# A second set of cell tiles, a planner fed with measured lengths, moved x tiles and paired output pieces in a fused retention and two-MLP kernel

## The chip, the cores and the metric

The kernel runs on one core of a Trainium2 chip. The metric is device time in microseconds (us), the median of several executions; lower is better. Durations inside the kernel come from one profiled execution.

## The reference, cut to what matters

Retention (linear attention with a decay per head) over 4 x 8 heads of 576 tokens, then two MLPs on the 2304 tokens that result, all in float32:

```python
ret = scores * Dmat            # scores = q k^T / 8, Dmat = gamma ** (i - j), lower triangle
x = (ret @ v)                  # 2304 tokens x 512
h = np.maximum(x @ w_in, 0.0)  # first MLP, 512 -> 2048 -> 512
x = h * h @ w_out
g = x @ w_gate                 # second MLP, 512 -> 1536 -> 512
out = g / (1 + exp(-g)) * (x @ w_val) @ w_out2
```

The weights arrive as float64 (the host only views them as 64-bit integers) and are rounded to float32 on the chip.

## The kernel before

Every float32 product is three TensorE matmuls: both operands are split into a high part, which is exact in the matmul's rounded format, and a low rest, and `three` (lines 188 to 190) adds high x high, high x low and low x high in PSUM.

**Tiles and stages.** The 2304 tokens are 18 cells of 128. Five token blocks (`BLOCKS`) of 4, 2, 4, 4 and 4 cells go through the first MLP.

- Start: the first four cells go through retention; PE fills planned idle time with matmuls on zeros (`fill`, line 1150).
- Stage 1: the plain blocks 0 (512 tokens) and 1 (256 tokens). For each of the 16 steps f of a block PE does 12 matmuls `h` (`mlp1_h`, into `hps`) and, one step later, 12 matmuls `y` (`mlp1_y`, into `acc`). After some of these steps one retention cell is inserted (`INSERTS`): `att_out` does I (previous state times q), K (sums k^T v, into `hps`) and O (decayed scores times v), and `att_scores` then does S, the scores of the next cell. Before, ten cells (4 to 13) stand in block 0, after f = 1, 3, 5, 7, 9, 11, 12, 13, 14, 15, and four in block 1. The scores of cell 4 stand directly ahead of its own I, K, O.
- Stage 2: blocks 2 to 4 by seven block products in place of eight (`mlp1_s`, `PRODUCTS`), eight double steps p a block. The moving operands are the `xb` tiles (256 columns); the seven products of a double step are followed in pairs by 512-column pieces of `y`.
- Stage 3: the second MLP in two-level form, 36 steps (`mlp2_gv`): seven products of six 384-column matmuls (`xc` tiles) a step, and six output pieces (`mlp2_o`, lines 1076 to 1078, 512 columns) of earlier steps, placed by `other(i)`: one piece before product 0, one after each of products 1 to 4, one after product 6, so that a lone piece stands on both sides of products 2 to 5, and two pieces stand together where one step meets the next.

**Cells and their tiles.** A cell needs three loads: `qk` (A, 512 KB), `kv` (V, 512 KB) and `qt` (Q, 256 KB), into one set of tiles in the pool `up`. The load of A for cell c waits for S and the q scaling (POOL, line 465) of cell c-1, Q for I of c-1, V for O and K of c-1. A cell's output is saved to DRAM (`xd`) from cell 6 on; all these saves stand ahead of the point `open`, from which stage 2's tiles take the room of the cells' tiles. `fetch_x1(2)` loads the first such block into `xs` and splits it into the seven `xb` tiles on ACT and DVE.

**Weights.** `round32` and `convert1` turn a raw 1 MB load into a split weight tile `w` (ACT lines 229, 234, 267; DVE lines 237, 240, 246, 249, 271); even ones are also stored to `wf` and later come back to `convert_s`, which forms the sums of the block products on POOL (line 337) and stores them in `ws`. Stage 2 converts the second MLP's weights (`convert_gv`, `convert_out`) to DRAM (`wdP`, `wdS`, `wdO`), from which stage 3 loads them through a ring of seven tiles.

**Order.** PE's order is written out by hand (`pe` chains each group to the one before). All other engines, SP (which issues the DMAs) included, get their order from `Plan`: a list scheduler that runs through the program with a length for each operation, takes for each engine the operation that is ready first, by rank, and emits it. The chip then runs each engine's queue in that order: an instruction, or a DMA issue, that has to wait holds up everything behind it on its engine. A DMA's planned landing is

```python
lanes = max(lanes, t + o.us + 1.3) + o.kb / 400.0
o.end = lanes + 0.5
```

**Addresses.** `pad` tiles shift what follows them. `x` of block 1 and the 256-column `h` tiles begin 192 bytes (`shift`, 48 floats) past a multiple of 1,024. The `xb` tiles follow the pools `pad2` to `tl` and `pad3`, which together put all their 1,024-byte parts at a multiple of 1,024.

In stage 3, product 6 writes the bank `MA` again and so waits for `c22` (DVE, line 1001), which reads product 4 from it.

Of the kernel before, what the change touches and what calls it, by code (L numbers as in the profile page):

```python
# [51 lines left out]
INSERTS = {0: (1, 3, 5, 7, 9, 11, 12, 13, 14, 15), 1: (1, 3, 5, 7)}  # L52
# [13 lines left out]
class Plan:  # L66
# [20 lines left out]
    def emit(self):  # L87
# [11 lines left out]
        while left:  # L99
# [45 lines left out]
def kernel(ctx: ExitStack, tc: tile.TileContext, units, qtab, tab, w1, w2, out):  # L145
# [24 lines left out]
    tl = ctx.enter_context(tc.tile_pool(name="tl", bufs=1))  # L170
    ctx.enter_context(tc.tile_pool(name="pad3", bufs=1)).tile([128, 80], F32, name="pad3")
# [50 lines left out]
    def round32(box, rank):  # L222
# [30 lines left out]
        p1 = do("DVE", 0.69, d1, [o1], rank)  # L253
        p2 = do("DVE", 0.69, d2, [p1], rank)
        p3 = do("DVE", 0.69, d3, [p2, o2], rank)
# [3 lines left out]
        p4 = do("DVE", 1.22, d4, [p3, o2], rank)  # L259
# [64 lines left out]
    def convert_s(p, rank):  # L324
# [16 lines left out]
        x = do("POOL", 0.67, add(2, 3, 2, ALU.add), [ld], rank)  # L341
        x = do("POOL", 0.67, add(3, 0, 3, ALU.subtract), [x], rank)
        x = do("POOL", 0.67, add(0, 2, 0, ALU.subtract), [x], rank)
        x = do("POOL", 0.67, add(1, 1, 0, ALU.subtract), [x], rank)
# [11 lines left out]
    def sums(st, deps, rank):  # L356
# [10 lines left out]
        s = do("POOL", 0.67, add(0, a21, a22, ALU.add, True), [*deps, *r_users[-1:]], rank)  # L367
        s = do("POOL", 0.67, add(1, 0, a11, ALU.subtract), [s], rank)
        s = do("POOL", 0.67, add(2, a11, a21, ALU.subtract), [s], rank)
        return do("POOL", 0.67, add(3, a12, 1, ALU.subtract), [s], rank)  # L370
# [23 lines left out]
    astack = ExitStack()  # L394
    xp = astack.enter_context(tc.tile_pool(name="xp", bufs=1))
# [29 lines left out]

    def att_load(c, rank):

        def go_a():
            A[c] = up.tile([128, NP, 2, C], F32, tag="qk", name="qk")
            nc.sync.dma_start(out=A[c], in_=units[c, 0])  # L430

        def go_b():
            V[c] = up.tile([128, NP, 2, C], F32, tag="kv", name="kv")
            nc.sync.dma_start(out=V[c], in_=units[c, 1])

        def go_q():
            Q[c] = up.tile([128, NP, C], F32, tag="qt", name="qt")
# [3 lines left out]
        A_op[c] = do("SP", 0.45, go_a, [S_op[c - 1], qs_op[c - 1]] if late_cell else (), rank, kb=512, after=[A_op[c - 1]])  # L441
        if c not in FIRST:
            Q_op[c] = do("SP", 0.45, go_q, [I_op[c - 1 - (c - 1 in FIRST)]] if late_cell else (), rank, kb=256, after=[Q_op[c - 1]])
        V_op[c] = do("SP", 0.45, go_b, [O_op[c - 1], K_op[c - 1]] if late_cell else (), rank, kb=512, after=[V_op[c - 1]])
# [11 lines left out]
    def att_prep(c, rank):  # L456
# [10 lines left out]
        if c not in FIRST:  # L467
            qs_op[c] = do("POOL", 1.3, qs, [A_op[c], Q_op[c]], rank, after=[ks_op[c - 1]])
        if c not in LAST:
            ks_op[c] = do("POOL", 1.15, ks, [V_op[c], tab_op], rank, after=[qs_op[c]])  # L470
# [23 lines left out]
    def att_out(c, rank, steps, fill=None, deps=()):  # L494
# [220 lines left out]
    def sum_loads():  # L715
# [5 lines left out]
        for n, (j, p, name, i) in enumerate(order):  # L721
# [4 lines left out]
            def go(j=j, p=p, name=name, k=k):  # L726
                if k == NF1P and "sx" not in late:
                    late["sx"] = late["xs"].tile([128, 2, HALF1], F32R, tag="sx", name="sx")
                SB[j, p, name] = t = Wt[2 * k][:, :, 3 * HALF1:] if k < NF1P else late["sx"]
# [13 lines left out]
    def mlp1_s(j, p, pieces):  # L743
# [58 lines left out]
        def finish(key, f, half, deps):  # L802
# [556 lines left out]
```

## Time and profile before

| | us |
|---|---|
| median of 3 runs (lowest, highest) | 932.97 (932.87, 933.08) |
| profiled execution, its own time | 934.24 |
| its span, first to last instruction | 932.5 |
| TensorE matmul (PE) busy | 895.4 |
| VectorE (DVE) busy | 561.7 |
| ScalarE (ACT) busy | 429.7 |
| GpSimd (POOL) busy | 193.0 |
| DMA, mean over the span | 253 GB/s |
| mean granted TensorE clock | 0.989 of full |

A share of busy time is a mean over the whole span; the stages have different limits. The start of a matmul to the start of the next is its price, since matmuls are pipelined and a row's duration overlaps the next one's. PE = TensorE matmul, SPq = the queue that issues DMAs.

### The profile page before, as it was taken

Reading aid. Unit: us, or ns where it says so; the run is one execution under the profiler, and the core shown is the slowest. Engines: PE = TensorE matmul, PEld = TensorE weight load, DVE = VectorE, ACT = ScalarE, POOL = GpSimd, SP = SyncE. Lnnn points to the kernel's source line nnn. Section 1 sums busy time; section 2 is a strip of 40 time slices with the busy share of each in tenths; the row PEclk is TensorE's granted clock in tenths of the full one; section 3 lists DMA queues with packets and bytes.
Section 4 is the critical chain, followed back from the end, with each engine's and each line's share of the span. In section 5 each row is a group of like instructions: output and inputs, shape, how many; then the busy total and the mean of one; then the engine's idle time right before and its main releaser. Section 6 shows DMA issues by size and latency. Waiting matters only on the chain.

```text
span 932.5 us, 14460 instructions
## 1 busy us (share of the span) xinstructions
PE 895.4 (96%) x5513; PEld 803.8 (86%) x5513; DVE 561.7 (60%) x841; ACT 429.7 (46%) x779; POOL 193.0 (21%) x213
## 2 busy tenths in 40 slices
PE   8799998989999999999999999999999999999998
PEld 6687877888899988988888889999999999999997
DVE  6888895534676865786677674447544445444444
ACT  3566763436566655666556442224322223322222
POOL 4121126441335443544442100000000000000000
PEclk9999999989999999999999999999999999999999
DMA  9678878987898797859788995555755555855541
GB/s 359 268 230 277 295 255 294 327 267 243 289 341 284 231 324 258 292 179 316 242 289 289 366 384 204 203 203 203 271 203 203 203 203 203 271 203 203 203 170 67
DMA packets 83620, 235.85 MB, mean 253 GB/s; under 512 B 7008, under 2 KB 38752, under 8 KB 71904
## 3 DMA queue, kind: packets, MB, share of 16 engines
q1 hardware_dynamic: 83552, 234.94, 71.2%
q8 instruction: 43, 0.70, 0.3%
q14 instruction: 25, 0.20, 0.1%
HBM read 181.44 MB, written 53.48 MB: 252 GB/s over the span
## 4 chain that ended last, share of the span: by engine, by line
PE 65%; DMA 17%; DVE 9%; ACT 4%; issue 2%; POOL 2%; SPq 1%; ACTq 0%; POOLq 0%; DVEq 0%
PE gv L188 11%; PE gv L190 11%; PE gv L189 11%; DMA wdS<-s 6%; PE acc L189 4%; PE acc L188 3%; PE acc L1077 3%; PE acc L190 3%; PE acc L1078 3%; PE acc L1076 3%; DMA wf<-f 3%; DVE f L249 2%; PE hps L188 2%; PE hps L189 1%; PE hps L190 1%
## 5 line engine op out<-in xcount | busy, mean ns | idle before, releaser
L189 PE MATMUL gv<-xc,w 128*128 128x384 f32 x504 | 170.5, 338 | 0.0
L190 PE MATMUL gv<-xc,w 128*128 128x384 f32 x504 | 170.1, 337 | 0.0
L188 PE MATMUL gv<-xc,w 128*128 128x384 f32 x504 | 169.0, 335 | 0.9 <-DVE m L1001 0.8
L189 PE MATMUL acc<-h,w 128*128 128x512 f32 (+1 forms) x320 | 120.0, 375 | 1.6 <-DVE h L623 1.5
L188 PE MATMUL acc<-h,w 128*128 128x512 f32 (+1 forms) x320 | 119.7, 374 | 0.5 <-ACT h L808 0.5
L190 PE MATMUL acc<-h,w 128*128 128x512 f32 (+1 forms) x320 | 118.3, 370 | 0.0
L1009 ACT ACTIVATE sg<-g 128x384 f32<-128x384 f32 x72 | 37.8, 525 | 157.9 <-DVE g L1004 121.8
L800 POOL TENSOR_TENSOR g<-g 128x256 f32<-128x256 f32 x96 | 81.4, 859 | 132.1 <-ACT g L796 130.7
L188 PEld LDWEIGHTS gv<-xc,w 128*128 128x128 f32 x504 | 94.7, 188 | 10.6 <-DVE m L1001 1.5
L189 PEld LDWEIGHTS gv<-xc,w 128*128 128x128 f32 x504 | 94.4, 187 | 8.2
L190 PEld LDWEIGHTS gv<-xc,w 128*128 128x128 f32 x504 | 94.7, 188 | 0.0
L1001 DVE TENSOR_TENSOR m<-gv,m 128x384 f32<-128x384 f32 x36 | 20.0, 556 | 100.6 <-PE gv L190 100.6
L190 PEld LDWEIGHTS acc<-h,w 128*128 128x128 f32 x320 | 61.0, 191 | 10.7
L189 PEld LDWEIGHTS acc<-h,w 128*128 128x128 f32 x320 | 61.2, 191 | 9.5 <-DVE h L623 2.3
L188 PEld LDWEIGHTS acc<-h,w 128*128 128x128 f32 x320 | 61.2, 191 | 8.0 <-ACT h L808 0.9
L188 PE MATMUL gv<-xb,w 128*128 128x256 f32 x222 | 64.1, 289 | 3.7 <-DVE g L790 2.9
L812 DVE TENSOR_TENSOR h<-g,h 128x256 fp32r<-128x256 f32 x96 | 55.0, 575 | 20.8 <-ACT h L808 20.8
L190 PE MATMUL gv<-xb,w 128*128 128x256 f32 x222 | 63.0, 284 | 0.0
L189 PE MATMUL gv<-xb,w 128*128 128x256 f32 x222 | 63.0, 284 | 0.0
L1076 PE MATMUL acc<-w,at 128*128 128x512 f32 x144 | 56.3, 391 | 1.9 <-DMA w<-wdO 1.9
L1078 PE MATMUL acc<-w,at 128*128 128x512 f32 x144 | 57.1, 397 | 0.0
L1077 PE MATMUL acc<-w,at 128*128 128x512 f32 x144 | 57.0, 396 | 0.0
(146 smaller groups left out, 1906.5 us busy)
## 6 DMA issues: line engine op xcount, KB each, us to landing
w<-wdS SPq DMA_DIRECT2D x36, 1024.0 KB, 6.2
raw<-w SPq DMA_DIRECT2D x34, 1024.0 KB, 7.0
w<-wdP SPq DMA_DIRECT2D x36, 768.0 KB, 6.3
w<-ws SPq DMA_DIRECT2D x85, 256.0 KB, 5.3
w<-wdO SPq DMA_DIRECT2D x18, 1024.0 KB, 4.8
ws<-cw SPq DMA_DIRECT2D x16, 512.0 KB, 5.7
qk<-units SPq DMA_DIRECT2D x14, 512.0 KB, 5.1
kv<-units SPq DMA_DIRECT2D x14, 512.0 KB, 5.0
```

The costliest lines, as they stand in the source:

```text
L188: nc.tensor.matmul(ps, lhsT=wh, rhs=xh, start=first, stop=False, skip_group_check=onto)
L189: nc.tensor.matmul(ps, lhsT=wh, rhs=xl, start=False, stop=False, skip_group_check=onto)
L190: nc.tensor.matmul(ps, lhsT=wl, rhs=xh, start=False, stop=last, skip_group_check=onto)
L249: nc.vector.tensor_tensor(out=st["f"], in0=st["f"], in1=st["r"], op=ALU.add)
L800: return lambda: nc.gpsimd.tensor_tensor(out=st[key][:, half], in0=st[key][:, half], in1=st[key][:, half], op=ALU.mult)
L812: nc.vector.tensor_tensor(out=t[:, 1, half], in0=st[key][:, half], in1=t[:, 0, half].bitcast(F32), op=ALU.subtract)
L1001: nc.vector.tensor_tensor(out=st["m5"], in0=late["MA"][:, :HALF], in1=st["m5"], op=ALU.add)
L1009: nc.scalar.activation(out=t, in_=st["g"][:, r], func=ACTF.Sigmoid)
L1076: nc.tensor.matmul(ps, lhsT=at[:, 0, sl], rhs=wh, start=f == 0, stop=False)
L1077: nc.tensor.matmul(ps, lhsT=at[:, 0, sl], rhs=wl, start=False, stop=False)
L1078: nc.tensor.matmul(ps, lhsT=at[:, 1, sl], rhs=wh, start=False, stop=f == NF2 - 1)
```

## The change

- **Cells.** Block 0 gets eight cells (4 to 11, every second f), block 1 six (12 to 17, after f = 1, 2, 4, 5, 7, 8). In block 1 every second cell takes its tiles from a second set (`place`), which lies in the room of block 0's x after that block's last `h`; loads there wait for the cell before last. The scores of cell 4 move one step forward, behind the first `h` of block 0.
- **Planned lengths.** DMA landings are planned 1.4 us later; the DVE steps of `round32` 0.8, 0.8, 0.87 and 1.34 in place of 0.69, 0.69, 0.69 and 1.22; POOL's additions and squares 0.87 for 0.67; the cells' POOL and PE steps longer as well.
- **Addresses.** `pad3` and the pool `tl` no longer stand below `xb`; `tl` is opened with stage 2 itself. The `xb` tiles come to lie 320 bytes lower, 704 bytes past a multiple of 1,024; `pad4`, `pad5` and a pool of its own for `sx` keep `sx` and the later tiles where they were.
- **Output pieces.** In stage 3 the six pieces stand in three pairs: after product 1, after product 3 and after product 6.

```diff
-INSERTS = {0: (1, 3, 5, 7, 9, 11, 12, 13, 14, 15), 1: (1, 3, 5, 7)}
+INSERTS = {0: (1, 3, 5, 7, 9, 11, 13, 15), 1: (1, 2, 4, 5, 7, 8)}
...
-                o.end = lanes + 0.5
+                o.end = lanes + 1.9
...
-    tl = ctx.enter_context(tc.tile_pool(name="tl", bufs=1))
-    ctx.enter_context(tc.tile_pool(name="pad3", bufs=1)).tile([128, 80], F32, name="pad3")
...
-        p1 = do("DVE", 0.69, d1, [o1], rank)
+        p1 = do("DVE", 0.8, d1, [o1], rank)
...
-        x = do("POOL", 0.67, add(2, 3, 2, ALU.add), [ld], rank)
+        x = do("POOL", 0.87, add(2, 3, 2, ALU.add), [ld], rank)
...
+    astack.enter_context(tc.tile_pool(name="pad3", bufs=1)).tile([128, 208], F32, name="pad3")
...
+    two = n0 + len(INSERTS[0])
+
+    def place(c, kind):
+        if c > two and (c - two) % 2:
+            if "cell" not in first:
+                first["cell"] = xp.tile([128, 20, C], F32, tag="x", name="cell")
+            lo, hi = {"qk": (0, 8), "kv": (8, 16), "qt": (16, 20)}[kind]
+            t = first["cell"][:, lo:hi]
+        else:
+            t = up.tile([128, 4 if kind == "qt" else 8, C], F32, tag=kind, name=kind)
+        return t if kind == "qt" else t.rearrange("p (a b) c -> p a b c", b=2)
...
-        A_op[c] = do("SP", 0.45, go_a, [S_op[c - 1], qs_op[c - 1]] if late_cell else (), rank, kb=512, after=[A_op[c - 1]])
+        o = c - 1 if c <= two else c - 2
+        q = o - (o in FIRST)
+        x0 = [h_op[0, NF1 - 1]] if c == two + 1 else []
+        A_op[c] = do("SP", 0.45, go_a, x0 or [S_op[o], qs_op[o]] if late_cell else (), rank, kb=512, after=[A_op[c - 1]])
...
-            qs_op[c] = do("POOL", 1.3, qs, [A_op[c], Q_op[c]], rank, after=[ks_op[c - 1]])
+            qs_op[c] = do("POOL", 1.45, qs, [A_op[c], Q_op[c]], rank, after=[ks_op[c - 1]])
...
-                I_op[c] = pe(0.5, inter, [qs_op[c], st_op[c - 1], xo_free], fill)
+                I_op[c] = pe(1.1, inter, [qs_op[c], st_op[c - 1], xo_free], fill)
...
-        other(0)
...
         product(1, "MB", [("c12", s - 1), ("s12", last2)])
...
+        other(0)
         other(1)
         product(2, "MA", [m1])
...
-        other(2)
         product(3, "MB", [c11_])
...
+        other(2)
         other(3)
         product(4, "MA", [u2_])
...
-        other(4)
         product(5, "MB", [m5])
...
         product(6, "MA", [c22_])
...
+        other(4)
         other(5)
...
     def swap():
         astack.close()
-        for key in ("xb", "xs"):
+        late["tl"] = ctx.enter_context(tc.tile_pool(name="tl", bufs=1, reuse_waits="tile"))
+        for key in ("xb", "xs", "pad4", "sx"):
...
-            if j == 0 and f == 1:
+            if j == 0 and f == 0:
                 att_scores(n0, rank)
```

## Rows read from the trace of the kernel before

**Rows 1.** The page's first part: busy us, share of span, instructions.
```profile
PE 895.4 (96%) x5513; PEld 803.8 (86%) x5513; DVE 561.7 (60%) x841; ACT 429.7 (46%) x779; POOL 193.0 (21%) x213
```

**Rows 2.** Stretches of the span: PE, PEld, DVE, ACT, POOL busy, clock, DMA.
```profile
40.00:60.00 20.00, 17.68 (x122) 14.68 (x121) 16.87 (x22) 11.36 (x14) 3.02 (x2) 0.91 0.72 238
140.00:240.00 100.00, 89.92 (x808) 82.78 (x807) 47.92 (x71) 42.94 (x83) 43.00 (x46) 0.93 0.82 272
480.00:500.00 20.00, 17.70 (x100) 15.40 (x99) 16.68 (x22) 11.37 (x26) 11.36 (x12) 0.91 0.89 282
560.00:900.00 340.00, 340.00 (x1766) 315.92 (x1765) 155.43 (x256) 105.31 (x191) 0.00 (x0) 1.00 0.59 215
```

**Rows 3.** Timeline of PE in stage 1: start, us, instruction [idle before <-releaser].
```profile
45.58 1.98 PE L515 MATMUL xs<-P,kv 128*64 128x128 f32 x16 [2.32 <-DVE P L488]
...
139.41 1.05 PE L504 MATMUL xs<-qt,state 128*128 128x128 f32 x8
...
142.97 0.50 PE L188 MATMUL hps<-x,w 128*128 128x512 f32 x1
...
153.69 1.16 PE L477 MATMUL sc<-qk 64*128 64x128 f32 x16 [2.56 <-DMA qk<-units]
...
196.69 2.08 PE L504 MATMUL xs<-qt,state 128*128 128x128 f32 x8 [3.14 <-POOL qt L465]
...
221.54 0.39 PE L188 MATMUL hps<-x,w 128*128 128x256 f32 x1 [2.02 <-ACT r L609]
```

**Rows 4.** Timeline of ACT just before PE's wait at 221.54.
```profile
220.59 0.62 ACT L267 CAST xb<-xs 128x512 fp32r<-128x512 f32 x1 [3.33 <-DMA xs<-xd]
```

**Rows 5.** Timeline of DVE and of PE around step 12 of block 0.
```profile
117.90 1.22 DVE L271 TENSOR_TENSOR w<-f,w 128x1024 fp32r<-128x1024 f32 x1
...
124.24 0.50 PE L188 MATMUL hps<-x,w 128*128 128x512 f32 x1 [0.83 <-DVE state L553]
```

**Rows 6.** Timeline of PE: 72 matmuls from `h` and x, 12 from `xb`.
```profile
227.38 0.28 PE L188 MATMUL acc<-h,w 128*128 128x256 f32 x1
...
235.54 0.28 PE L188 MATMUL acc<-h,w 128*128 128x256 f32 x1
...
277.29 0.28 PE L188 MATMUL gv<-xb,w 128*128 128x256 f32 x1
...
278.72 0.40 PE L188 MATMUL acc<-h,w 128*128 128x512 f32 x1
```

**Rows 7.** Waits of PE over the span: us in total, times, longest.
```profile
PE hps L188 <- ACT m L783: 3.2, 3, 2.2
...
PE gv L188 <- DVE g L790: 2.9, 4, 1.0
...
PE acc L1076 <- DMA w<-wdO: 1.9, 2, 1.2
```

**Rows 8.** Timeline of PE, products 5 and 6 of a step of stage 3.
```profile
582.89 0.39 PE L1076 MATMUL acc<-w,at 128*128 128x512 f32 x1
583.59 0.33 PE L188 MATMUL gv<-xc,w 128*128 128x384 f32 x1
...
584.65 0.33 PE L188 MATMUL gv<-xc,w 128*128 128x384 f32 x1
...
585.69 0.39 PE L1076 MATMUL acc<-w,at 128*128 128x512 f32 x1
586.39 0.39 PE L1076 MATMUL acc<-w,at 128*128 128x512 f32 x1
587.08 0.33 PE L188 MATMUL gv<-xc,w 128*128 128x384 f32 x1
```

**Rows 9.** Timeline of DVE and PE: `c22` in that step, and in step 2.
```profile
583.16 0.56 DVE L1001 TENSOR_TENSOR m<-gv,m 128x384 f32<-128x384 f32 x1 [3.57 <-PE gv L190]
...
536.68 0.55 DVE L1001 TENSOR_TENSOR m<-gv,m 128x384 f32<-128x384 f32 x1
...
537.28 0.44 PE L188 MATMUL gv<-xc,w 128*128 128x384 f32 x1 [0.83 <-DVE m L1001]
```

More of the change, by code (lines that the diff above doesn't have):

```diff
@@ L252, in round32 @@
         o2 = do("ACT", 1.16, a2, [o1, *r_users[-1:]], rank)
-        p1 = do("DVE", 0.69, d1, [o1], rank)
-        p2 = do("DVE", 0.69, d2, [p1], rank)
-        p3 = do("DVE", 0.69, d3, [p2, o2], rank)
+        p1 = do("DVE", 0.8, d1, [o1], rank)
+        p2 = do("DVE", 0.8, d2, [p1], rank)
+        p3 = do("DVE", 0.87, d3, [p2, o2], rank)
         raw_free = do("NONE", 0.0, lambda: None, [o2, p3])
@@ L258, in round32 @@
         converts.append(o1)
-        p4 = do("DVE", 1.22, d4, [p3, o2], rank)
+        p4 = do("DVE", 1.34, d4, [p3, o2], rank)
         r_users.append(p4)
@@ L366, in sums @@
         a21, a11, a12, a22 = (slice(256 * i, 256 * i + 256) for i in range(4))
[L367 to L370, printed above, removed]
+        s = do("POOL", 0.87, add(0, a21, a22, ALU.add, True), [*deps, *r_users[-1:]], rank)
+        s = do("POOL", 0.87, add(1, 0, a11, ALU.subtract), [s], rank)
+        s = do("POOL", 0.87, add(2, a11, a21, ALU.subtract), [s], rank)
+        return do("POOL", 0.87, add(3, a12, 1, ALU.subtract), [s], rank)
     def convert_gv(box, f, rank):
@@ L467, in att_prep @@
         if c not in FIRST:
-            qs_op[c] = do("POOL", 1.3, qs, [A_op[c], Q_op[c]], rank, after=[ks_op[c - 1]])
+            qs_op[c] = do("POOL", 1.45, qs, [A_op[c], Q_op[c]], rank, after=[ks_op[c - 1]])
         if c not in LAST:
-            ks_op[c] = do("POOL", 1.15, ks, [V_op[c], tab_op], rank, after=[qs_op[c]])
+            ks_op[c] = do("POOL", 1.25, ks, [V_op[c], tab_op], rank, after=[qs_op[c]])
     def att_scores(c, rank, fill=None):
@@ L726, in go @@
             def go(j=j, p=p, name=name, k=k):
-                if k == NF1P and "sx" not in late:
-                    late["sx"] = late["xs"].tile([128, 2, HALF1], F32R, tag="sx", name="sx")
-                SB[j, p, name] = t = Wt[2 * k][:, :, 3 * HALF1:] if k < NF1P else late["sx"]
+                SB[j, p, name] = t = Wt[2 * k][:, :, 3 * HALF1:] if k < NF1P else late["S"]
                 nc.sync.dma_start(out=t.bitcast(F32), in_=ws_dram[p][:, ("S2", "S4", "S1", "S3").index(name)])
@@ L781, in go @@
             def go():
-                st[key] = tl.tile([128, HALF1], F32, tag=key, name=key)
+                st[key] = late["tl"].tile([128, HALF1], F32, tag=key, name=key)
                 nc.scalar.copy(out=st[key], in_=tiles[bank][:, :HALF1])
@@ L812, in lo @@
                 nc.vector.tensor_tensor(out=t[:, 1, half], in0=st[key][:, half], in1=t[:, 0, half].bitcast(F32), op=ALU.subtract)
-            r = do("POOL", 0.67, square(key, half), deps, -2)
+            r = do("POOL", 0.87, square(key, half), deps, -2)
             h = do("ACT", act, hi, [r, y_op.get(order1[i - 2])], -2)
-            return do("DVE", dve, lo, [h], -2)
+            return do("DVE", 0.58, lo, [h], -2)
         product(0, "MA", [("s21", *prev), "open", relu_op[PLAIN_BLOCKS - 1, NF1 - 1]])
@@ L991, in go @@
             def go():
-                st[name] = tl.tile([128, HALF], F32, tag=name, name=name)
+                st[name] = late["tl"].tile([128, HALF], F32, tag=name, name=name)
                 nc.scalar.copy(out=st[name], in_=late[bank][:, :HALF])
@@ L1206, in swap @@
         astack.close()
-        for key in ("xb", "xs"):
+        late["tl"] = ctx.enter_context(tc.tile_pool(name="tl", bufs=1, reuse_waits="tile"))
+        for key in ("xb", "xs", "pad4", "sx"):
             late[key] = bstack.enter_context(tc.tile_pool(name=key, bufs=7 if key == "xb" else 1, reuse_waits="tile"))
+        late["pad4"].tile([128, 80], F32, name="pad4")
+        late["S"] = late["sx"].tile([128, 2, HALF1], F32R, tag="sx", name="sx")
         pgv = ctx.enter_context(tc.tile_pool(name="pgv", bufs=1, space=PSUM, reuse_waits="tile"))
@@ L1219, in swap3 @@
         bstack.close()
-        for key, bufs in (("xl", NXL), ("ys", 1)):
+        for key, bufs in (("pad5", 1), ("xl", NXL), ("ys", 1)):
             late[key] = ctx.enter_context(tc.tile_pool(name=key, bufs=bufs, reuse_waits="tile"))
+        late["pad5"].tile([128, 80], F32, name="pad5")
     pend = None
```

18 lines of the change are left out of this document (9 added, 9 removed).

## Prediction, made before the changed kernel was run

> **What bounds the kernel now.** I read the page's busy shares first: PE's matmuls are busy 895.4 of 932.5 us, the next engine 561.7 [rows 1]. So PE is the bound, and only two things can shorten the kernel: idle time and half-clock time of PE, and a lower price of a matmul. Then I read stretches of the span. From 560 to 900 PE is busy for all of 340.00 us at a clock of 1.00 [rows 2]: the last 36-step stage has no wait left, only the price of its matmuls. From 140 to 240, where the last retention cells stand, PE is idle for 10 of 100 us and the mean clock is 0.93. The clock has two levels, 2.4 and 1.2 GHz, and time at half clock counts half, so a mean of 0.93 over 100 us is a loss of about 7 us. Two more stretches have 0.91 over 20 us, a loss of 1.8 us each [rows 2].
>
> The timeline of PE names the waits in the first of these places [rows 3]: 2.32 us for cell 4's decayed scores (DVE), and three waits of 2 us and more later, 2.56 (the load of the next cell's `qk`), 3.14 (the q scaling on POOL, which had to wait for its turn and its loads) and 2.02 (a relu on ACT). The reader is to see that each is a wait for something that a cell's single set of tiles delays, but for the last: there ACT had stood 3.33 us on a copy into `xb` that waited for a load of `xs`, with the relu queued behind it [rows 4].
>
> **Cells, block 0.** With cell 4's scores one step earlier, a whole step (h(1) and y(0)) lies between them and cell 4's O, so the 2.32 us go, and with them the clock loss of 1.8 us in that stretch [rows 2, 3]. The scores themselves then run in the gap in which PE waits for the first relu; a cell costs 142.97 - 139.41 = 3.56 us for four parts [rows 3], so a quarter of it, 0.9 us, is saved at most. That makes 5.0 us. The work is only moved: what it can meet is the weights. At step 12 the weight tile is complete at 117.90 + 1.22 = 119.12, and PE asks for it at 124.24 [rows 5]: PE can come 5.1 us earlier and no more, as long as the conversions keep their pace. I take 5.0; bounds 3 (a conversion step that slips, or half of these savings eaten by the 0.83 us state wait there) and 8 (conversions earlier too, since DVE has two cells less to serve).
>
> Moving two cells from block 0 to block 1 moves 2 x 3.56 us of PE's work and removes nothing.
>
> **Cells, block 1.** The three waits are 2.56 + 3.14 + 2.02 = 7.7 us, and the clock loss of 140 to 240 another 7.0: 14.7 together [rows 2, 3]. With two sets the loads of cell c wait for cell c-2, so they have one whole cell interval more, in a schedule where cells follow each other after one or two steps. The third wait hangs on the load of `xs`, which stands behind the stores of `convert_s`; these in turn wait for the tile in which block 0's output is saved, and that is free earlier by as much as block 0 ends earlier (two cells and more). New waits that I see: cell 12 still takes the single set from cell 11, two PE steps before; and the stretch gets shorter with the same bytes. At 272 GB/s over these 100 us and a DMA share of 0.82 [rows 2], the same transfers in 84 us would need about 320 GB/s and a share of 0.98: landings will be late here and there. SP's queue adds to it: a load of A, Q or V that waits at its head holds up the `wf` loads, `ws` stores and saves behind it. I leave 4 us of waits and clock loss and take 10.7. Bounds: 16 (all of it and the waits under 2 us) and 4 (loads late again, and half clock after them).
>
> **Planned lengths.** They cost nothing by themselves; they reorder ACT, DVE, POOL and SP. In stage 2 PE's own waits are on the copies (ACT, 3.2 us) and sums (DVE, 2.9 us) of the products, with one loss of clock of 1.8 us at 480 to 500 [rows 2, 7]: 7.9 us, where an engine stood on something that waits for a DMA while a short piece that PE needs was queued behind it. Planning landings 1.4 us later puts such instructions later in the queues. I take 2 of the 7.9; bounds a gain of 7 and a loss of 4 (other collisions take their place; the order of every queue changes). At the start the planned landings lengthen the zero matmuls before the first scores: 0.4 us lost, bounds 0 and 1.4 (all of the added landing).
>
> **Addresses.** The nearest rows are matmuls of the same 256 columns. From `h` and block 1's x, 192 bytes past a multiple of 1,024, 72 of them take 235.54 - 227.38 = 8.16 us, 113.3 ns each; from `xb`, at a multiple, 12 take 278.72 - 277.29 = 1.43 us, 119.2 ns each [rows 6]. Weights and form are alike. The new place, 704, is 192 + 512, and is not in the trace. All 72 at 192 have one price although their weight slices step by 512 bytes, so I take 704 to be as good as 192. Stage 2 has 3 blocks x 8 x 7 x 6 = 1,008 such matmuls: 1,008 x 5.9 ns = 5.9 us. Bounds 0 (a step of 512 in the moving tile does matter) and 6.
>
> Here the Trainium skill, page "TensorE: Matmul & The Clock Gate", section "Part 2: What happens when you issue a matmul", speaks against the change: it gives start-to-start as N / 2.4 + 2.5 ns, 109 ns for 256 columns by its figures, and says that moving data and weights have independent read ports, so that an address would change nothing. By it the sum would lack these 5.9 us. The trace does not agree that the place is indifferent, 113.3 against 119.2 [rows 6].
>
> **Pieces in pairs.** In a step of stage 3 product 5, between two pieces, takes 584.65 - 583.59 = 1.06 us; product 6, behind another product, 1.04. A lone piece takes 0.70, the second of a pair 586.39 to 587.08, 0.69 [rows 8]. With pairs no product stands between lone pieces: products 2 to 5 save 0.02 each, two pieces 0.01 each, 0.10 us a step, times 34 full steps 3.4 us. Bounds 0 (product 2 and 4 keep their price behind a pair, and so on) and 4.
>
> What the pairs take away is cover: product 6 waits for `c22`, and only product 5 stands between. Product 5 would start at 582.89, where the piece now does, and product 6 at 583.95; `c22` ends at 583.16 + 0.56 = 583.72 [rows 8, 9]. PE starts 0.05 us after it (536.68 + 0.55 = 537.23, 537.28 in step 2) [rows 9], so 0.18 us are to spare, and the cost is nothing. Where `c22` is late anyway, as in step 2, the wait grows by a piece, 0.7 us: twice, 1.4 us. Against it, the first output pieces come after product 6, two products or 2.1 us later, and the 1.9 us of waits for `wdO` [rows 7] are covered. Net 0.5 gained; bounds 2 gained, 3 lost.
>
> **Sum.** 5.0 + 10.7 + 2.0 - 0.4 + 5.9 + 3.4 + 0.5 = 27.1 us. Against the profiled execution's own 934.24 that is 907.1; the median of the runs, 932.97, lies 1.3 lower, so 905.8: I say **906**. Less than 0.2%, 1.9 us, is what a measurement of this kernel cannot tell from no change.
>
> **Rivals.**
>
> 1. *The address does nothing at 704.* For it: no row at 704, and the page's rule. Against it: rows 6. All else stays, 906 + 5.9 = 912.
> 2. *Block 1 keeps its waits.* The loads are earlier but the DMA is full, so loads or POOL's queue end up late; each wait of some 2 us is followed by half clock. For it: the share of 0.98 worked out above. Against it: a whole interval of lead. Only 4 of the 10.7 come: 906 + 6.7 = 913.
> 3. *Slower: `c22` sets the pace of stage 3.* DVE takes other work ahead of it in each step, because the plan sees `c22` later than it is. Two DVE instructions of 0.56 us ahead make it 1.12 late, less 0.18 to spare, 0.94 x 34 = 32 us: 906 + 32 = 938. It decides from (27.1 / 34) + 0.18 = 0.98 us of lateness a step. Against it: DVE stood idle 3.57 us before `c22` [rows 9], and is under half busy from 560 to 900 (155.43 of 340) [rows 2].
> 4. *More.* Conversions come earlier too and block 1 has no wait: 8 in place of 5.0 and 16 in place of 10.7: 906 - 8.3 = 898.
>
> **How the numbers follow.** Forecast, within 6 us of 906: 0.45. Rival 1: 0.15. Rival 2: 0.20. Rival 4: 0.15. Rival 3: 0.03. The rest, 0.02, several losses at once near no change. The range goes from 894 (rival 4 with its own 4 us below) to 918 (rivals 1 and 2 together, 918.6); outside lie rival 3, the rest and the edges, under 2 in 10. Faster by over 0.2%: all but rival 3 and part of the rest, 0.95; within 0.2% 0.01; slower 0.04.
>
> **What would show it.** Right: 256-column matmuls from `xb` at 113 ns; products 2 to 5 at 1.04 us and steps 0.10 us shorter; no wait on `c22` between 560 and 900; step 2 of block 0 about 5 us earlier; the clock of the stretch of the last cells near 0.98; the first block product 16 us earlier. Wrong: `xb` matmuls at 119; a wait before product 6 in each step; waits on `w` (DVE L271) in block 0 that hold PE to its old times; PE waits on `qk`, `qt` or `xs` in block 1 of 2 us and more.

## The result: 894.3 us against 932.9, and the profile after

The changed kernel takes 894.32 us in the median (893.61 to 897.10, 4 runs), the kernel before 932.92 in the same comparison (931.22 to 933.08, 4 runs). The ratio is 0.9596, 95% interval 0.9573 to 0.9619. The forecast was 906 with a range from 894 to 918: the time lies at the range's lower edge, and the gain is 38.6 us where 27.1 were worked out.

The profiled execution took 894.44 us, its span 892.6. The page's first part (busy us, share of the span, instructions):

```profile
PE 876.4 (98%) x5517; PEld 793.4 (89%) x5517; DVE 560.3 (63%) x841; ACT 432.7 (48%) x779; POOL 182.7 (20%) x213
```

PE does the same work in 19.0 us less of busy time [rows 1] and stands still 20.9 us less (932.5 - 895.4 = 37.1 before, 16.2 now). Part of the busy time is clock: a matmul at half clock counts as busy for about twice as long (512 columns: 0.43 us against 0.23, in scores_late below). Stretches of the span, in the columns of [rows 2]:

```profile
40.00:60.00 20.00, 20.00 (x158) 16.95 (x156) 17.65 (x24) 12.58 (x17) 2.35 (x2) 1.00 0.78 261
140.00:240.00 100.00, 96.05 (x912) 89.73 (x911) 58.02 (x88) 51.40 (x107) 44.90 (x51) 1.00 0.94 327
...
560.00:860.00 300.00, 299.50 (x1565) 277.88 (x1564) 140.94 (x230) 97.46 (x174) 0.00 (x0) 1.00 0.63 230
```

The clock is 1.00 in each of them; where the last cells stand it was 0.93 [rows 2]. The DMA share there rose to 0.94 at 327 GB/s; 0.98 and 320 were worked out. From 560 on PE still has next to no wait. Waits of PE over the span (us in total, times, longest):

```profile
PE xs L520 <- DVE state L571: 2.4, 1, 2.4
PE hps L1164 <- DVE wz L1147: 1.4, 1, 1.4
PE gv L187 <- DVE xb L269: 1.3, 1, 1.3
...
PE gv L186 <- DVE g L804: 0.5, 1, 0.5
PE gv L186 <- ACT m L1007: 0.5, 1, 0.5
PE acc L1090 <- DMA w<-wdO: 0.5, 1, 0.5
PE gv L186 <- ACT u L797: 0.4, 1, 0.4
```

In the whole view no line names `qk` or `qt` any more. The copies and sums of stage 2's products, 3.2 and 2.9 us before [rows 7], are down to 0.4 (L797) and 0.5 (L804), the wait for `wdO` from 1.9 to 0.5.

Four starts from PE's timeline cut the span into stages: step 12 of block 0, the first matmul of block 1, the first block product, the first of stage 3. The DVE line is the weight tile of step 12, answering to [rows 5].

```profile
118.40 0.50 PE L186 MATMUL hps<-x,w 128*128 128x512 f32 x1
...
147.61 0.39 PE L186 MATMUL hps<-x,w 128*128 128x256 f32 x1
...
216.21 0.28 PE L186 MATMUL gv<-xb,w 128*128 128x256 f32 x1
...
464.26 0.33 PE L186 MATMUL gv<-xc,w 128*128 128x384 f32 x1
```
```profile
112.13 1.21 DVE L269 TENSOR_TENSOR w<-f,w 128x1024 fp32r<-128x1024 f32 x1
```

From such starts, before and after (block 0 lost two cells, 7.1 us, to block 1; both cells' places taken together, that cancels):

| stretch of PE | before, us | after, us | change | forecast |
|---|---|---|---|---|
| start, to the first `h` of block 0 | 30.35 | 32.30 | +1.95 | +0.4 |
| blocks 0 and 1, to the first `xb` product | 207.41 | 183.91 | -23.5 | -5.0 - 10.7 = -15.7 |
| stage 2, to the first `xc` product | 263.66 | 248.05 | -15.6 | -5.9 - 2.0 = -7.9 |
| stage 3, to the last matmul | 427.30 | 424.63 | -2.7 | -3.4 - 0.5 = -3.9 |
| behind it | 3.74 | 3.74 | 0 | 0 |
| sum | | | -39.8 | -27.1 |

The sum is that of the two profiled executions (934.24 - 894.44 = 39.8). The miss sits in two lines: 7.8 us in blocks 0 and 1 and 7.7 in stage 2, less 1.6 at the start and 1.2 in stage 3. The start differs from one execution of this kernel and its variants to the next (29.95 to 32.30 in the profiles below), so its 1.95 is not a stage to explain.

### The profile page after: what moved, and what is told of

Same layout as the page of the kernel before. It is cut to its first block, busy times and chain, and to the rows that moved or that the text cites. A ratio compares the mean times of both kernels' runs of the same rounds, so it can differ in the third digit from the quotient of the medians.

```text
span 892.6 us, 14473 instructions
## 1 busy us (share of the span) xinstructions
PE 876.4 (98%) x5517; PEld 793.4 (89%) x5517; DVE 560.3 (63%) x841; ACT 432.7 (48%) x779; POOL 182.7 (20%) x213
## 4 chain that ended last, share of the span: by engine, by line
PE 88%; DMA 5%; DVE 3%; issue 1%; ACT 1%; POOL 1%; SPq 0%; POOLq 0%; DVEq 0%; ACTq 0%
PE gv L186 12%; PE gv L187 12%; PE gv L188 12%; PE acc L187 7%; PE acc L188 7%; PE acc L186 7%; PE hps L186 4%; PE acc L1092 3%; PE acc L1091 3%; PE hps L187 3%; PE acc L1090 3%; PE hps L188 3%; DMA wdS<-s 2%; PE sc L493 1%; PE xs L531 1%
## 5 line engine op out<-in xcount | busy, mean ns | idle before, releaser
L187 PE MATMUL acc<-h,w 128*128 128x512 f32 (+1 forms) x320 | 117.7, 368 | 0.7 <-DVE h L826 0.7
L188 PE MATMUL acc<-h,w 128*128 128x512 f32 (+1 forms) x320 | 117.5, 367 | 0.0
L186 PE MATMUL acc<-h,w 128*128 128x512 f32 (+1 forms) x320 | 117.4, 367 | 0.0
L814 POOL TENSOR_TENSOR g<-g 128x256 f32<-128x256 f32 x96 | 75.2, 796 | 146.7 <-ACT g L810 146.5
L188 PEld LDWEIGHTS acc<-h,w 128*128 128x128 f32 x320 | 60.1, 188 | 9.9
L187 PEld LDWEIGHTS acc<-h,w 128*128 128x128 f32 x320 | 60.1, 188 | 7.5 <-DVE h L826 1.0
L826 DVE TENSOR_TENSOR h<-g,h 128x256 fp32r<-128x256 f32 x96 | 52.8, 554 | 21.5 <-ACT h L822 21.0
L186 PEld LDWEIGHTS acc<-h,w 128*128 128x128 f32 x320 | 60.1, 188 | 6.3
L186 PE MATMUL gv<-xb,w 128*128 128x256 f32 x222 | 62.8, 283 | 0.9 <-DVE g L804 0.5
L187 PE MATMUL gv<-xb,w 128*128 128x256 f32 x222 | 62.5, 281 | 1.3 <-DVE xb L269 1.3
L188 PE MATMUL gv<-xb,w 128*128 128x256 f32 x222 | 62.4, 281 | 0.0
```

What stands on the lines that cost most here:

```text
L186: nc.tensor.matmul(ps, lhsT=wh, rhs=xh, start=first, stop=False, skip_group_check=onto)
L187: nc.tensor.matmul(ps, lhsT=wh, rhs=xl, start=False, stop=False, skip_group_check=onto)
L188: nc.tensor.matmul(ps, lhsT=wl, rhs=xh, start=False, stop=last, skip_group_check=onto)
L814: return lambda: nc.gpsimd.tensor_tensor(out=st[key][:, half], in0=st[key][:, half], in1=st[key][:, half], op=ALU.mult)
L826: nc.vector.tensor_tensor(out=t[:, 1, half], in0=st[key][:, half], in1=t[:, 0, half].bitcast(F32), op=ALU.subtract)
```

## The experiments

Each is the changed kernel with one edit, but for the one with the lengths alone, which is the kernel before with one part of the change. The ratio is always to the kernel before. Stages are worked out from the first matmuls of each, as above: block 0 / block 1 / stage 2 / stage 3. The changed kernel has 115.3 / 68.6 / 248.0 / 424.6, the kernel before 135.3 / 72.1 / 263.7 / 427.3.

| label | median, us | ratio (95%) | stages |
|---|---|---|---|
| changed kernel | 894.3 | 0.9596 (0.9573, 0.9619) | 115.3 / 68.6 / 248.0 / 424.6 |
| one_set | 919.2 | 0.9850 (0.9808, 0.9892) | 115.4 / 93.3 / 250.7 / 422.9 |
| scores_late | 904.8 | 0.9698 (0.9667, 0.9730) | 121.7 / 71.1 / 248.5 / 425.2 |
| old_inserts | 900.1 | 0.9647 (0.9605, 0.9690) | 127.5 / 60.8 / 248.1 / 424.1 |
| old_lengths | 911.1 | 0.9762 (0.9713, 0.9811) | 120.1 / 68.9 / 260.9 / 422.2 |
| only_lengths | 915.7 | 0.9815 (0.9762, 0.9868) | 132.8 / 66.8 / 253.1 / 426.0 |
| old_landing | 913.5 | 0.9816 (0.9764, 0.9868) | 121.0 / 74.4 / 257.0 / 424.0 |
| landing_2_9 | 905.6 | 0.9717 (0.9690, 0.9744) | 115.6 / 69.3 / 255.6 / 428.9 |
| xb_at_0 | 897.1 | 0.9612 (0.9568, 0.9656) | 115.4 / 68.3 / 252.8 / 423.4 |
| right_192 | 900.8 | 0.9647 (0.9596, 0.9698) | 115.9 / 68.3 / 254.1 / 426.2 |
| right_192_xb_192 | 899.4 | 0.9645 (0.9584, 0.9705) | 115.9 / 68.6 / 254.2 / 424.4 |
| lone_pieces | 895.7 | 0.9615 (0.9554, 0.9676) | 115.4 / 67.3 / 248.0 / 426.5 |

Besides the kernel before, only the profiles old_inserts and only_lengths have ten cells in block 0; their block 0 compares with 115.3 + 7.1 = 122.4.

### The second set of tiles

**One set again**, with the changed places of the cells:

```diff
-        if c > two and (c - two) % 2:
+        if False:
...
-        o = c - 1 if c <= two else c - 2
+        o = c - 1
...
-        x0 = [h_op[0, NF1 - 1]] if c == two + 1 else []
+        x0 = []
```

> The changed kernel with one set of cell tiles in block 1 (the loads of a cell wait for the cell before it again). Theory (the second set hides the loads, which come every one or two steps in block 1): waits on qk, qt or kv of 2 us and more for most of the five cells, each with half clock behind it, 8 to 15 us: 903 to 909. Rival (planned landings and the even spread are enough): 894 to 897.

919.2 us: the second set is worth 24 to 25 us here, more than was expected. Block 1 alone is 24.7 us longer. Waits of PE from 145 to 245:

```profile
PE xs L520 <- POOL qt L481: 9.1, 3, 5.7
PE sc L493 <- DMA qk<-units: 6.0, 3, 2.5
```

The two lines, 15.1 us, are loads of cells and the scalings that wait for them, the kinds that PE had before [rows 3]; the rest of the 24.7 is smaller waits and half clock behind them (the mean clock over block 1 is 0.87). With cells after one or two steps, one set can't be reloaded in time; with two the same places cost no such wait at all.

### Where the cells stand in block 0

**Scores of cell 4 late again:**

```diff
-            if j == 0 and f == 0:
+            if j == 0 and f == 1:
                 att_scores(n0, rank)
```

> The changed kernel with the scores of cell 4 directly ahead of its I, K, O again (after h(1) instead of h(0)). Theory 1 (block 0's saving of 12.9 us comes in good part from this move): the wait of about 2 us for the decayed scores (DVE) and the half clock behind it are back, step 2 is 3 to 4 us later and the whole 4 to 6 us longer, 898 to 900. Theory 2 (with the measured lengths DVE makes the scores in time anyhow, as in the kernel before with the lengths alone, where the wait was 0.4): 0.5 to 2 us longer, 895 to 896.5.

904.8 us, some 10 over the changed kernel: more than either theory. Block 0 is 6.4 us longer, block 1 2.5. But the wait is another one. Timeline of PE:

```profile
45.00 1.09 PE L531 MATMUL xs<-P,kv 128*64 128x128 f32 x16 [0.43 <-DVE P L504]
48.20 2.08 PE L493 MATMUL sc<-qk 64*128 64x128 f32 x16 [2.11 <-DMA qk<-units]
...
51.23 0.63 PE L188 MATMUL hps<-x,w 128*128 128x512 f32 x1
...
53.79 0.63 PE L188 MATMUL hps<-x,w 128*128 128x512 f32 x1
...
54.54 0.39 PE L187 MATMUL hps<-x,w 128*128 128x512 f32 x1
54.77 0.39 PE L188 MATMUL hps<-x,w 128*128 128x512 f32 x1
```

The decayed scores come only 0.43 us late, where the kernel before had waited 2.32 [rows 3]. It is the load of the next cell's `qk` that comes 2.11 late. That load waits for the tile that these scores read, so late scores mean a late issue, as SP's timeline shows, first here and then in the changed kernel:

```profile
42.98 0.33 SPq L443 DMA_DIRECT2D qk<-units  x1
```
```profile
37.59 0.33 SPq L443 DMA_DIRECT2D qk<-units  x1
```

5.4 us earlier, though this kernel's block 0 begins 1.0 us later (32.30 against 31.30): the move of one cell's scores takes the wait from the loads of the next cell, too. Behind the wait the matmuls of 512 columns run at half clock: from 51.23 to 53.79 there are six, 0.43 us each, and from 54.54 to 54.77 one takes 0.23.

**The old places of the cells**, with two sets:

```diff
-INSERTS = {0: (1, 3, 5, 7, 9, 11, 13, 15), 1: (1, 2, 4, 5, 7, 8)}
+INSERTS = {0: (1, 3, 5, 7, 9, 11, 12, 13, 14, 15), 1: (1, 3, 5, 7)}
```

> The changed kernel with the ten and four cells of before, so the last four cells of block 0 stand after steps 12, 13, 14, 15 again; two sets of tiles stay for block 1. Theory 1 (block 0 is short because no two cells follow each other after one step): block 0 has waits for loads again and is 4 to 6 us longer than 115.3 and the two cells, block 1 has no wait and the whole is 897 to 902. Theory 2 (the places don't matter with the new lengths): block 0 is 122.4, the first xb product again near 216, and the whole 894 to 896.

900.1 us, some 5 more, as the first theory said: block 0 is 127.5 long, 5.1 over the 122.4 that it would be with two more cells, and block 1 has no more to give (60.8 against 68.6 - 7.1 = 61.5). The places after each of the steps 12 to 15 cost these 5 us even with later planned landings.

### The planned lengths

**All lengths and landings as before**, in the changed kernel:

```diff
-                o.end = lanes + 1.9
+                o.end = lanes + 0.5
...
-        p1 = do("DVE", 0.8, d1, [o1], rank)
+        p1 = do("DVE", 0.69, d1, [o1], rank)
...
-        x = do("POOL", 0.87, add(2, 3, 2, ALU.add), [ld], rank)
+        x = do("POOL", 0.67, add(2, 3, 2, ALU.add), [ld], rank)
...
```

> The changed kernel, planned with the lengths and landings of the kernel before; cells, places and pairs as changed. Theory (the measured lengths removed the waits of stage 2 and part of those of block 1): PE's waits in stage 2 go from 2.9 back to about 9 us with a stretch of half clock, and block 1 gets one or two waits of 2 us back: 905 to 912. Rival (the second set and the earlier start of stage 2 removed them, the lengths only shuffle): 893 to 897.

911.1 us, some 16 more; 12.9 of it are in stage 2.

**The lengths and landings alone**, in the kernel before: the same lines of the diff the other way round, and nothing else of the change.

> The kernel before with the planned lengths and landings of the changed one and nothing else. Theory (the lengths by themselves remove waits of stage 2 wherever stage 2 starts): PE's waits in stage 2 fall from 9.2 to 3 or 4 us and its half clock goes, stage 2 is 8 to 11 us shorter; the single set keeps block 1 as it was: 921 to 926. Rival (the lengths help only together with the cells' second set, which frees the queues): 930 to 935.

915.7 us, 18 us less than the kernel before in the same comparison (933.7), where 921 to 926 were expected. Stage 2 is 10.6 us shorter, with the `xb` tiles where they were; and block 0 is 2.5 and block 1 5.3 us shorter (132.8 and 66.8 against 135.3 and 72.1), with one set of tiles and the old places. From both sides, then, this part is worth 16 to 18 us, of which I had taken 2.0 - 0.4.

**The landing alone as before**, the longer instructions kept:

```diff
-                o.end = lanes + 1.9
+                o.end = lanes + 0.5
```

> The changed kernel with landings planned at lanes + 0.5 again; the longer lengths of DVE, POOL and PE stay. All lengths and landings put back together cost about 17 us (block 0, first xb 4.9 later, stage 2 12.9 longer). Theory 1: the landings carry most of it, because a queue only stands when an instruction that waits for a DMA is put ahead of others: 906 to 911, stage 2 near 260 and the clock dips back. Theory 2: the lengths carry most of it, because they are what lets engines drift against the plan: 896 to 899, stage 2 near 250 and no dip. Both alike: 900 to 905.

913.5 us: with the landings put back nothing is left of that gain. With the old landings the longer lengths of DVE, POOL and PE bring no gain that can be seen (913.5 with them, 911.1 without); the new landings with the old lengths were not run. What an early landing does, ACT's timeline of this kernel shows, and PE's right behind it:

```profile
216.16 1.12 ACT L227 ACTIVATE f<-raw 128x1024 f32<-128x1024 f32 x1 [3.77 <-DMA raw<-w]
217.18 0.61 ACT L265 CAST xb<-xs 128x512 fp32r<-128x512 f32 x1
217.69 0.39 ACT L625 ACTIVATE r<-hps 128x256 f32<-128x256 f32 x1
```
```profile
218.12 0.39 PE L186 MATMUL hps<-x,w 128*128 128x256 f32 x1 [2.96 <-ACT r L625]
```

The plan saw the raw weights landed and put the conversion `f` ahead; on the chip ACT stands on it for 3.77 us with the relu `r` (0.39 us of work) in the queue behind, and PE stands for 2.96. It is the pattern of [rows 4], with another load. Summed over ACT's waits that end with a DMA, the kernel before has 46.6 us, old_landing 72.7, the changed kernel 33.3.

**The landing another 1.0 us later:**

```diff
-                o.end = lanes + 1.9
+                o.end = lanes + 2.9
```

> The changed kernel with landings planned another 1.0 us later (lanes + 2.9). In the trace of the changed kernel a 1,024 KB load lands 6.7 to 7.0 us after its issue, a 512 KB load 6.0 to 8.2; the plan with idle lanes says 5.8 and 4.5, so it is still early. Theory 1: the closer the planned landing to the measured one, the fewer the waits, and more of the gain is to be had: start about 1 us longer, stage 2 within 1 us of 245 and stage 3 below 424, the whole 889 to 893. Theory 2: with 1.9 the queues already hold nothing that waits for long; what is left of the waits (2.9 us in stage 2, 2.5 in stage 3) hangs on PE's own results, and another plan only deals the collisions anew: 893 to 898.

905.6 us, 11 us slower than with 1.9, and neither theory's number. ACT's waits on DMAs do fall, to 19.0 us, as the first theory had it. But two that are left stand where they hurt. ACT and PE at the start of stage 2:

```profile
220.16 0.40 ACT L822 CAST h<-g 128x256 fp32r<-128x256 f32 x1 [1.17 <-POOL g L814]
221.98 1.12 ACT L227 ACTIVATE f<-raw 128x1024 f32<-128x1024 f32 x1 [1.42 <-DMA raw<-w]
223.00 2.17 ACT L265 CAST xb<-xs 128x512 fp32r<-128x512 f32 x4
```
```profile
223.66 0.58 PE L186 MATMUL gv<-xb,w 128*128 128x256 f32 x1 [5.07 <-ACT xb L265]
```

The casts that make the next `xb` tiles stand behind `h`, which waited for POOL, and `f`, which waited for a load. PE stands 5.07 us, and then runs at half clock (a mean of 0.50 from 222.5 to 229.2). The same happens with `xc` at the start of stage 3 (a wait of 3.37 us, then 0.50 from 478.5 to 485.2). So 1.9 is not a value on a slope: ACT's waits fall with a later plan (72.7, 33.3, 19.0 us at 0.5, 1.9 and 2.9), but which piece stands behind the waiting one is dealt anew, and the two waits named here, with the half clock behind them, make up most of the loss. Three values were tried; how much of the gain at 1.9 is a better match with the landings and how much a lucky order is not shown. Not every landing was planned too early either: the `wdO` loads, 1,024 KB too, land after 4.8 us, before the 5.8 of the plan.

### The addresses

**`xb` back at a multiple of 1,024 bytes:**

```diff
-        for key in ("xb", "xs", "pad4", "sx"):
+        for key in ("pad6", "xb", "xs", "sx"):
...
-        late["pad4"].tile([128, 80], F32, name="pad4")
+        late["pad6"].tile([128, 80], F32, name="pad6")
```

> The changed kernel with the xb tiles moved back up by 320 bytes, to a multiple of 1,024; nothing else differs, the queues' order included. Theory (the place of the moving tile sets the price of the matmuls): the 1,008 xb matmuls go from 117.6 back to 119.2 ns and the 576 pieces of y between them from 227 back to 231 ns, so stage 2 is longer by 1.7 + 2.3 = 4 us and the time is 898. Rival (stage 2 is faster only because its waits are gone, the place does nothing): prices stay at 117.6 and 227, time 894, within 1 us.

897.1 us, whose interval takes in the changed kernel's ratio; in the profiles stage 2 is 4.8 us longer (252.8 against 248.0), and the argument rests on that. `xs`, from which `xb` is cut, moves with it. Timelines of PE in stage 2, first this kernel (eight matmuls from `xb`, then six of `y`), then the changed one (six of `y`, then eight from `xb`):

```profile
228.22 0.28 PE L186 MATMUL hps<-xb,w 128*128 128x256 f32 x1
...
229.18 0.28 PE L188 MATMUL gv<-xb,w 128*128 128x256 f32 x1
229.30 0.40 PE L186 MATMUL acc<-h,w 128*128 128x512 f32 x1
...
230.69 0.28 PE L186 MATMUL hps<-xb,w 128*128 128x256 f32 x1
```
```profile
228.52 0.39 PE L186 MATMUL acc<-h,w 128*128 128x512 f32 x1
...
229.88 0.28 PE L186 MATMUL hps<-xb,w 128*128 128x256 f32 x1
...
230.82 0.28 PE L188 MATMUL gv<-xb,w 128*128 128x256 f32 x1
```

A matmul from `xb` costs (229.18 - 228.22) / 8 = 0.120 us here and (230.82 - 229.88) / 8 = 0.1175 in the changed kernel; over stage 2 the means are 119.7 and 118.2 ns. The 113 of the forecast does not come. But the `y` pieces between the products, whose own tiles did not move, cost (230.69 - 229.30) / 6 = 0.232 and (229.88 - 228.52) / 6 = 0.227 us; the means are 231.7 and 227.0. 1,008 x 1.5 ns + 576 x 4.7 ns = 1.5 + 2.7 = 4.2 us, close to the 4.8 measured.

**Three places side by side**: the 256-column `h` tiles of block 1 at 704, 0 and 192 bytes past a multiple of 1,024 for f = 0, 1, 2, and so on in turn (one run with a profile).

```diff
-            t = hp.tile([128, 2 * n + shift(n)], F32R, tag="h", name="h")
-            Hs[j, f] = t[:, shift(n):].rearrange("p (a n) -> p a n", a=2)
+            cut = 0 if n == 512 else (176, 0, 48)[f % 3]
+            t = hp.tile([128, 2 * n + cut], F32R, tag="h", name="h")
+            Hs[j, f] = t[:, cut:].rearrange("p (a n) -> p a n", a=2)
```

> The changed kernel with the 256-column h tiles of block 1 at three places in turn: 704 bytes past a multiple of 1,024 (f = 0, 3, 6, ...), at a multiple (f = 1, 4, ...), and at 192 as before (f = 2, 5, ...). Same instructions, same weights, one price each to read. Theory 1 (704 is a dearer place than 192): y at 704 takes 117 to 118 ns as the xb matmuls do, at 192 113, at 0 119 to 120. Theory 2 (a step of 512 does not matter, and the block products are dear for another reason): y at 704 takes 113 as at 192, at 0 119 to 120. The time moves by under 1 us either way.

898.7 us in a single execution, so the time is not weighed; only the prices count. First and last matmul of `y` for f = 10 (at 0), 11 (at 192) and 12 (at 704):

```profile
204.79 0.28 PE L186 MATMUL acc<-h,w 128*128 128x256 f32 x1
...
206.09 0.28 PE L188 MATMUL acc<-h,w 128*128 128x256 f32 x1
...
207.59 0.28 PE L186 MATMUL acc<-h,w 128*128 128x256 f32 x1
...
208.83 0.28 PE L188 MATMUL acc<-h,w 128*128 128x256 f32 x1
...
210.31 0.28 PE L186 MATMUL acc<-h,w 128*128 128x256 f32 x1
...
211.55 0.28 PE L188 MATMUL acc<-h,w 128*128 128x256 f32 x1
```

Eleven intervals each: 1.30, 1.24 and 1.24 us, 118, 113 and 113 ns. Over all 16 steps it is 118 to 119 ns at 0 and 113.4 at 192 and 704, but for f = 0 (at 704) with 117.7, which it also has in the changed kernel, at 192. So 704 is as good as 192, as the forecast took it; what makes `xb` dearer is something else.

**The weights moved.** All weight tiles (with them stage 3's `xc` tiles and ring) by 192 bytes, with `h`, x and `xb` where they are; then the same with `xb` 512 bytes higher, at 192 past a multiple of 1,024.

```diff
-    pad.tile([128, 248], F32, name="pad")
+    pad.tile([128, 200], F32, name="pad")
```

> The changed kernel with the last pad of 992 bytes cut to 800, so that every weight tile, the xc tiles and the ring lie 192 bytes further up, while x, h and xb stay. Theory 1 (the moving tile's own place sets the price): stage 1's 256-column matmuls stay at 113, the output pieces, whose moving operand is a weight tile, go from 231.6 to 227 ns (648 x 4.6 = 3 us) and the xc matmuls from 174.5 to 172 or less: 887 to 891. Theory 2 (the distance between moving and weight tile sets it): stage 1's 256-column matmuls, at the weights' place now, rise to 119, xb changes too, the output pieces and xc do not gain: 895 to 900.

> The same cut of the last pad, and the 192 bytes used to put xb at 192 past a multiple of 1,024 (with sx at 192 too). Theory 1 (own place): xb at 113 to 114 in place of 117.6, 1,008 x 4 = 4 us less than the run with the cut alone: 883 to 888. Theory 2 (distance to the weights): xb at the weights' own place, 119 to 120, 2 us more than the run with the cut alone.

900.8 and 899.4 us, stage 2 at 254.1 and 254.2. In both, every `y` of block 1 costs 120.0 ns, though its `h` lies at 192 as before; `xb` costs 120.0 and 120.2, the `y` pieces of stage 2 234.1 and 234.0. For the 256-column matmuls, then, not the place of the moving tile by itself counts, but its place relative to the weights. A step of 512 bytes in `xb`, all that differs between the two, changes nothing.

### The output pieces

**Lone pieces again** in stage 3, as in the diff, the other way round.

> The changed kernel with the six output pieces of a step where they stood before: one ahead of product 0, one after each of products 1 to 4, one after product 6. Theory (a product between lone pieces costs 0.02 us more, and pieces in pairs come late enough for the wdO loads): steps of 11.55 us in place of 11.47, 0.085 x 34 = 2.9 us more, and about 2 us more in the first four steps, less up to 2 us of waits that steps 4 to 13 have only with pairs: 896 to 899. Rival (the pairs' gain is eaten by waits on c22 and copies in steps 4 to 13): 893 to 895.

895.7 us, whose interval takes in the changed kernel's ratio. In the profiles stage 3 is 426.5 against 424.6: 1.9 us, and that is all that can be said of this part.

## Why the prediction was right, and where its sizes were off

**Direction and mechanism held.** PE stayed the bound; the gain came from its waits, its half clock and its prices, in the stages named. Rival 2 (block 1 keeps its waits) and rival 3 (`c22` sets the pace) did not happen: block 1 has no wait on `qk` or `qt` left at a DMA share of 0.94, and from 560 on PE waits 0.2 us for `c22`, once, and 300 us hold 299.50 us of matmuls. One term was far too small, the planned lengths. That the time still lies in the range is partly luck: the low edge came from rival 4, more gain in the cells, and most of the surplus came by another way.

**Block 0, 5.0 us.** The term itself held: from the first `h` to step 2 block 0 takes 49.28 - 30.35 = 18.93 us before and 46.69 - 32.30 = 14.39 after, 4.5 less. Step 2, before and after:

```profile
49.28 0.50 PE L188 MATMUL hps<-x,w 128*128 128x512 f32 x1
```
```profile
46.69 0.50 PE L186 MATMUL hps<-x,w 128*128 128x512 f32 x1
```

All of block 0 gained 12.9 us (135.3 - 115.3, less the two cells' 7.1). Of the rest, 3.3 lie between steps 2 and 12. There waits for `state` (DVE) of 1.6 and 0.8 us are gone, as they are with the lengths alone: steps 3 to 12 take 69.4 us in the kernel before, 66.1 in only_lengths and in the changed kernel. And 5.1 lie from step 12 on, where four cells stood after every step; old_inserts loses 5 us with these places. Two more readings of mine were off here:

- The conversions are no cap. I let PE come 5.1 us earlier at step 12, to 119.12 [rows 5]; it came to 118.40, and the tile was complete at 112.13 + 1.21 = 113.34. The conversion moved forward as far as PE did (119.12 - 113.34 = 5.8 us, 124.24 - 118.40 = 5.8), and its lead stayed 5.1. In all profiles here the lead is 3.7 to 5.8 us, and PE waits for no `w` in block 0: the conversions did not pace PE. That they follow it is likely, not shown. This is rival 4's condition, conversions earlier too, which I gave 0.15.
- I costed only the waits that a step removes at its own place. The earlier scores also free the `qk` tile, and its next load is issued 5.4 us earlier: in scores_late that load's lateness of 2.11 us and the half clock behind it are most of block 0's loss of 6.4.

**Block 1, 10.7 us**: seen alone it is 72.1 + 7.1 - 68.6 = 10.6 us shorter than it would be, but the agreement is partly luck. My 10.7 counted the 2.56 us for `qk` at 153.69 [rows 3] and the half clock behind it, which lie in block 0 (block 1 begins at 165.66) and which no second set reaches; and the planned lengths alone, with one set, make block 1 5.3 us shorter (put back in the changed kernel they cost it 0.3, the landings alone 5.8). What the second set is worth, one_set shows: without it the new places cost 24.7 us.

**The planned lengths, 2.0 - 0.4 us, were the step that failed**: they brought 16 to 18 us, by undoing and by doing them alone, beyond my bound of 7. With the landings alone put back nothing of it is left. I had the mechanism (a waiting instruction at the head of a queue, a short piece behind it), and its bound of 7.9 us in stage 2; I took a quarter of it because a new order may deal new collisions, and I put it at nothing in blocks 0 and 1.

- In stage 2 without the addresses 15.6 - 4.8 = 10.8 us came (10.6 in only_lengths): PE's gaps there, summed over the timeline, fell from 9.2 to 2.9 us, the loss of clock of 1.8 us is gone, and the mean price of `xb` at its old place fell from 121.1 to 119.7 ns, 1.4 us. The bound was too low, since I read it from two lines of the view of waits [rows 7] and not from all gaps of the stage.
- In blocks 0 and 1 the lengths alone bring 2.5 + 5.3 = 7.8 us; putting them back in the changed kernel costs 4.8 + 0.3 = 5.1. Together the two blocks gained 23.5, so 15.7 to 18.4 are left for the cells, against 5.0 + 10.7 = 15.7. That the sum comes near rival 4's 8 + 16 is not rival 4's doing.

That the doubt about new collisions was not empty, landing_2_9 shows: a plan 1 us later yet loses 11 us.

**The addresses, 5.9 us**: 4.2 to 4.8, but not as worked out. 1,008 matmuls were to gain 5.9 ns each; they gained 1.5, and the rest came from `y` pieces that I had not counted. The step that failed is the price at the new place. I took 113.3 from 72 matmuls in one stretch [rows 6]; in the same block of the same kernel, with tiles at the same place and at the full clock, 24 matmuls take (207.41 - 204.59) / 24 = 0.1175 us:

```profile
204.59 0.28 PE L188 MATMUL acc<-h,w 128*128 128x256 f32 x1
...
207.41 0.28 PE L188 MATMUL acc<-h,w 128*128 128x256 f32 x1
```

So there were two levels before the change already, and `xb` at 704 runs mostly at the higher one. Rival 1, that 704 does nothing, fell with h_three_places and the longer stage 2 of xb_at_0, and with it what I had concluded from the Trainium skill. Its page "TensorE: Matmul & The Clock Gate", section "Part 2: What happens when you issue a matmul", has independent read ports for moving data and weights, and its formula N / 2.4 + 2.5 ns gives an estimate of 109 ns for 256 columns, with no term for where the tiles lie. The runs do not agree: they have 113 to 120 ns, in part by where moving tile and weights lie to each other.

**Pairs, 3.4 + 0.5 us**: 2.7 for the stage, 1.9 by lone_pieces. The price is right: in a step of the changed kernel product 0 takes 606.57 to 607.61 and product 2, behind a pair, 610.04 to 611.08, 1.04 us each as foretold:

```profile
606.57 0.33 PE L186 MATMUL gv<-xc,w 128*128 128x384 f32 x1
...
607.61 0.34 PE L186 MATMUL gv<-xc,w 128*128 128x384 f32 x1
...
610.04 0.33 PE L186 MATMUL gv<-xc,w 128*128 128x384 f32 x1
...
611.08 0.33 PE L186 MATMUL gv<-xc,w 128*128 128x384 f32 x1
```

A step without waits takes 11.47 us, from the end of one `c22` to the next, where it took 11.55: 0.08, just the four products, where 0.10 was worked out. Over 34 steps that is 2.7. The waits gained and lost (1.4 for `wdO`, against new ones for `m` and `u`) leave 0.4 of gaps less, 3.1 together; the stage shows 2.7.

The parts undone one at a time add up to more than the whole: by their ratios 23.7 + 15.5 + 9.5 + 4.8 + 1.5 + 1.8 = 56.8 us against 38.6. They cover for each other: the denser cells need the second set (one_set), and where a wait of 2 us or more comes back, half clock comes with it (scores_late, landing_2_9). The price of a part holds in the company of the others.

## What to carry to other kernels

Where a planner fixes the order of in-order queues, check its DMA landings against the trace before anything else: planning them 1.4 us earlier cost 16 to 20 of 933 us here, since an instruction that waits for a load holds up short pieces that the bound engine needs; but try several values, for another 1.0 us later cost 11. And cost such a change in every stage whose engines the planner orders, not only in the one whose waits you have read. When a step is moved forward, follow the tile that it frees to the next load. And of each engine that seems to cap the bound one, ask whether it paces it or follows it. A price read from one stretch of a trace may be one of two levels: read it over the whole stage.

## What the runs showed of the hardware that was not expected

- The interval between matmuls depends on where the moving tile and the weights lie to each other: 256 columns at 113 ns or 118 to 120, with the moving tile alone (h_three_places) or the weights alone (right_192) moved by 192 bytes.
- At one and the same distance there are two levels, at the full clock. The first product from `xb` in the changed kernel runs at 113 to 114 ns, and after a wait the next ones at 117 to 118:

```profile
216.33 0.28 PE L187 MATMUL gv<-xb,w 128*128 128x256 f32 x1
...
217.46 0.28 PE L188 MATMUL gv<-xb,w 128*128 128x256 f32 x1
...
219.87 0.39 PE L187 MATMUL gv<-xb,w 128*128 128x256 f32 x1 [1.27 <-DVE xb L269]
...
220.21 0.28 PE L186 MATMUL gv<-xb,w 128*128 128x256 f32 x1
...
220.91 0.28 PE L186 MATMUL gv<-xb,w 128*128 128x256 f32 x1
```

  Ten intervals of 1.13 us in all, 113 ns, then six of 0.70, 117 ns. The wait alone does not set the level: in block 1 of the same profile `y`, with its tiles at 192, takes 117.8 ns from 183.75 to 194.37 and 113.5 from 197.98, while PE is busy for all 15.00 us from 183 to 198; and `xb` itself is back at 113.4 from 224.87 and at 117.8 from 226.45, with no wait between. What sets it, and why the `y` pieces of stage 2 gain 4.7 ns when `xb` moves, stays open; no run here separates it.
